# Block products summed in PSUM banks, and q's relu and weighting moved to GpSimd, in a fused attention and SwiGLU kernel

## The chip, the cores and the metric

The kernel runs on one core of one Trainium2 chip. The metric is the device time of one execution in microseconds. A core has TensorE (PE, matrix products), VectorE (DVE), ScalarE (ACT), GpSimd (POOL) and SyncE (SP, which here only issues transfers); each runs its own queue of instructions in order, and they wait for one another through semaphores. TensorE writes only into PSUM, eight banks of 128 partitions by 512 float32 values.

## The reference

Eight batches of eight heads, 576 positions, 64 features. A linear attention with cosine weights, whose result feeds a gated feed-forward network:

```python
theta = pi / 2 * arange(S) / S
phi(x) = concat([relu(x) * cos(theta), relu(x) * sin(theta)])   # 64 -> 128 features
q_p, k_p = phi(q), phi(k)
kv  = einsum('bhsf,bhsd->bhfd', k_p, v);   z = sum of k_p over s
x   = einsum('bhsf,bhfd->bhsd', q_p, kv) / (einsum('bhsf,bhf->bhs', q_p, z) + 1e-6)
g   = x @ w_gate                      # x as 4608 tokens of 512
out = (silu(g) * (x @ w_val)) @ w_out # 512 -> 1536 -> 512
```

## The kernel before

**Tokens and groups.** The 4608 tokens are taken in nine groups (`tg` = 0 to 8) of 512 tokens, four tiles `t` of 128 each. A batch has 576 tokens, four and a half tiles, so batches and groups drift apart. One group is twelve steps `ffn_fc(tg, fc)` and then the output product. A step multiplies the group's transposed tokens `xT[tg]` by 128 columns of the gate and of the value weights (L531: two PSUM banks, eight matmuls of 128x512), ACT takes silu of the one bank (L537), and DVE multiplies it by the other into `ht` (L542).

**The output by seven products.** For groups 2 to 8 `out_by_quarters` forms the output `ht @ w_out` as a two by two block product with seven block products in place of eight, in Winograd's form. Each `product` is 12 matmuls of 128x256 (L648) over six chunks. The sums of blocks of `ht` (S1 to S4) are formed by DVE in `token_sum` (L619), those of the weights (T1 to T4) once. In program order the products are: aq00·bq00 into bank `a`; S3·T3 into `e`; S2·T2 into `b`; aq10·bq10 on top of `a`; S1·T1 on top of `b`; aq11·T4 into `c`; S4·bq11 on top of `b`. The quarters of the output stand in SBUF tiles `ob` as C11, C12, C21 and C22. ACT copies `a` out twice, as C12 (L661, a part of the later sums) and as C11 (L672). `added` (L655) is DVE's scalar_tensor_tensor, PSUM times 2^-12 plus an SBUF block: five times in a group, C22 = e + C12, C21 = b + C22, C22 = b + C22, C21 = c + C21, C12 = b + C12. Each is a read of a bank that a later product may only write after it. In the last group `b` is two banks and its additions are halved.

**PSUM.** `take` hands out banks by least recent use; a bank with a `hold` stays taken until `give_back`.

**Attention work between the steps.** A plan written by hand (`at(slot, function)`) puts the attention's work for later batches into numbered slots, 16 for each group: twelve behind the `ffn_fc` steps, four inside the output product (`slot_of(0)` to `slot_of(3)`). For batches 4 to 7, in slots 12, 12, 13 and 14 of a group, `phi_q(b, g)` has ACT take relu of a quarter of q in place (L234) and DVE multiply it by the table of cosines and sines `tab` into `r_q` (L251; the tile pool `rel` has one buffer). In slots 15 and 16 SP issues `qturn_dma`: two transposing transfers of `r_q` into `phit` (L274). In slots 15 to 18 come relu of k (ACT, L234) and `vmul` (DVE, L255). The group 2 works for batch 4, group 3 for 5, group 4 for 6 and group 5 for 7. `a_tile2` (L415) multiplies `phit` by the state for the tiles of the next group, DVE normalises (`x_of`, L425 to L438), and SP transposes x into `xT` (L515).

**Loads.** POOL's queue issues the loads of q, k and v, 576 KB each. `load_behind(b)` first copies two values out of `phit` of batch b − 1 (L850), which makes POOL wait until those transposes have landed, and then issues q, k and v of batch b (L107). SP's queue holds the stores of `ob` (L570), the transposes L274 and the transposes L515, in that order from the end of one group to the next.

Of the kernel before, what the change touches and what calls it, by code (L numbers as in the profile page):

```python
# [11 lines left out]
BF16 = mybir.dt.bfloat16  # L12
FP16 = mybir.dt.float16
AF = mybir.ActivationFunctionType
ALU = mybir.AluOpType
# [3 lines left out]
def kernel(  # L19
# [10 lines left out]
    nc = tc.nc  # L30
    B, H, S, D = q.shape
    P = 128
    G = H // 2
    J = G // 2
    SH = 64
    NC = S // SH
# [9 lines left out]
    UP = float(2 ** 12)  # L46
    DOWN = 1.0 / UP
    HC = FC // 2
    HT = T // 2
    HD = d_model // 2  # L50
# [3 lines left out]
    rel = ctx.enter_context(tc.tile_pool(name="rel", bufs=1))  # L54
# [13 lines left out]
    now = [0]  # L68
    held = {}

    def take(n, hold=None):

        taken = {x for r in held.values() for x in r}
        free = [b for b in range(0, 8, n) if not any(b <= x < b + n for x in taken)]

        b0 = min(free, key=lambda b: (n == 1 and hold is not None and hold[0] == "o" and b ^ 1 not in taken,
                                      sorted(used[b:b + n], reverse=True)))
        if hold is not None:
            held[hold] = range(b0, b0 + n)
        touch(range(b0, b0 + n))  # L80
        return banks[:, b0] if n == 1 else banks[:, b0:b0 + n]

    def touch(r):
        now[0] += 1
        for x in r:
            used[x] = now[0]
# [5 lines left out]
    raws = {}  # L92
# [36 lines left out]
    first = {"q": lodge(G * QCUT * D, FP32).rearrange("p (g c d) -> p g c d", g=G, c=QCUT)}  # L129
# [25 lines left out]
    for j in range(2):  # L155
        t = consts.tile([P, 8 * J * D1], BF16, name=f"kvd_{j}")
# [8 lines left out]
    def idle_products(n, cols=P):  # L165
        ps = take(1)[:, 0:4 * cols]
        for _ in range(n):
# [22 lines left out]
                            op0=ALU.mult, op1=ALU.add)  # L190
# [4 lines left out]
    csk, cst = cs_all[:, 0], cs_all[:, 1]  # L195
# [7 lines left out]
        out=tab.rearrange("p c e d -> p (c e) d"),  # L203
        in_=csk.rearrange("p c e -> p (c e)").to_broadcast([P, NC * 2, D]),
    )
    v2s = []
    for j in range(2):
        t = consts.tile([P, G, NC, 2, W], BF16, name=f"v2_{j}")
# [21 lines left out]
    st = {}  # L230
# [14 lines left out]
    def phi_q(b, g):  # L245

        if g == 0:
            st[b, "q"] = rel.tile([P, G, NC, 2, D], BF16, name="r_q")
        o = raws[b, "q"][:, g]
        relu_op("act", o, o)  # L250
        nc.vector.tensor_tensor(out=st[b, "q"][:, g], in0=o.unsqueeze(2).to_broadcast([P, NC, 2, D]),  # L251
                                in1=tab, op=ALU.mult)

    def vmul(b, g):
        nc.vector.tensor_tensor(  # L255
# [262 lines left out]
    def ffn_mm(tg, fc, lo=0, hi=GH, which=(0, 1)):  # L518

        n = (hi - lo) * SH  # L520
        ts = slice(lo // 2, hi // 2)
        fs = slice(fc * P, (fc + 1) * P)
        if 0 in which:
            if 2 * n <= 512:
                both = take(1, ("f", tg, fc, lo))
                st["f", tg, fc, lo] = [both[:, 0:n], both[:, n:2 * n]]
            else:
                st["f", tg, fc, lo] = [take(1)[:, 0:n] for _ in range(2)]
        for i in which:
            for kc in range(KC):  # L530
                nc.tensor.matmul(out=st["f", tg, fc, lo][i], lhsT=(wg_sb, wv_sb)[i][:, kc, fs], rhs=xT[tg][:, ts, kc],  # L531
                                 start=(kc == 0), stop=(kc == KC - 1))
# [24 lines left out]
    o_ps = {}  # L557
# [23 lines left out]
    def ffn_out(t, f0=0, f1=None):  # L581

        f1 = FC if f1 is None else f1
        if f0 == 0:
            o_ps[t] = take(1, ("o", t))
        r = t % OUT * P
        for fc in range(f0, f1):
            nc.tensor.matmul(out=o_ps[t], lhsT=ht[:, fc, r:r + P], rhs=wo_sb[:, fc],  # L588
                             start=(fc == 0), stop=(fc == FC - 1))
        if f1 < FC:  # L590
            return
        ps = o_ps.pop(t)
        give_back(("o", t))
        if t % 2 == 0:
            nc.scalar.mul(out=ob_of(t), in_=ps, mul=DOWN)
        else:
            nc.vector.tensor_single_scalar(out=ob_of(t), in_=ps, scalar=DOWN, op=ALU.mult)
        store(t)


    aq = ht.rearrange("p (i w) (h t) -> p w h i t", w=2, h=2)
    bq = wo_sb.rearrange("p (i w) (h x) -> p w h i x", w=2, h=2)
    sums = consts.tile([P, 3, HC, HT], FP16, name="sums")
    S1, S2, S3, S4 = aq[:, 0, 1], sums[:, 0], sums[:, 1], sums[:, 2]
# [21 lines left out]
    def out_by_quarters(tg, slot_of):  # L626

        last = tg == NTG - 1
        t0 = tg * OUT
        for t in (t0, t0 + 2):  # L630
            ob_of(t)
        C11, C12 = (obs[t0 // 2][:, :, x * HD:(x + 1) * HD] for x in range(2))
        C21, C22 = (obs[t0 // 2 + 1][:, :, x * HD:(x + 1) * HD] for x in range(2))

        def home(nm, parts=1):
            return [take(1, ("o", tg, nm, i)).rearrange("p (t x) -> p t x", x=HD) for i in range(parts)]

        def free(nm, parts=1):
            for i in range(parts):
                give_back(("o", tg, nm, i))  # L640

        def at_of(x, i):
            return x[i][:, 0] if len(x) == 2 else x[0][:, i]

        def product(to, a, b, first):
            for i in range(2):
                for kc in range(HC):
                    nc.tensor.matmul(out=at_of(to, i), lhsT=a[:, kc, i * P:(i + 1) * P], rhs=b[:, kc],  # L648
                                     start=first and kc == 0 and (i == 0 or len(to) == 2),
                                     stop=kc == HC - 1, skip_group_check=True)  # L650

        def added(o, ps, x):
            for i in range(len(ps)):
                sl = slice(i, i + 1) if len(ps) == 2 else slice(0, 2)
                nc.vector.scalar_tensor_tensor(out=o[:, sl], in0=ps[i][:, 0:1] if len(ps) == 2 else ps[i],  # L655
                                               scalar=DOWN, in1=x[:, sl], op0=ALU.mult, op1=ALU.add)

        nb = 2 if last else 1
        a = home("a")
        product(a, aq[:, 0, 0], bq[:, 0, 0], True)  # L660
        nc.scalar.mul(out=C12, in_=a[0], mul=DOWN)  # L661
        e = home("e")
        product(e, S3, T3, True)
        added(C22, e, C12)
        b = home("b", nb)
        free("e")
        product(b, S2, T2, True)
        added(C21, b, C22)
        token_sum(4, 4, 6)
        slot_of(0)  # L670
        product(a, aq[:, 1, 0], bq[:, 1, 0], False)
        nc.scalar.mul(out=C11, in_=a[0], mul=DOWN)  # L672
        free("a")
        if last:
            store_two(t0, slice(0, HD))
        slot_of(1)
        product(b, S1, T1, False)
        added(C22, b, C22)
        if last:
            store_two(t0 + 2, slice(HD, d_model))  # L680
        c = home("c")
        product(c, aq[:, 1, 1], T4, True)
        added(C21, c, C21)
        free("c")
        if last:
            store_two(t0 + 2, slice(0, HD))
        else:
            for t in (t0 + 2, t0 + 3):
                store(t)
        slot_of(2)  # L690
        product(b, S4, bq[:, 1, 1], False)
        added(C12, b, C12)
        free("b", nb)
        for t in (t0, t0 + 1):
            store(t, *((slice(HD, d_model), (nc.sync, nc.scalar)) if last else ()))
        slot_of(3)
# [6 lines left out]
    hold = consts.tile([P, 1], FP32)  # L703
# [144 lines left out]
    def load_behind(b):  # L848

        nc.gpsimd.tensor_copy(out=hold2, in_=phit[b - 1][0:1, :, 0, 0, 0])  # L850
        load(b, "q")
        if b > 3:
            load_kv(b)

    def load_kv(b):
        for nm in ("k", "v"):
            load(b, nm)
# [7 lines left out]
    for b in range(2, B):  # L865
        s0 = SLOTS * (b - 1)
        keng = "dve" if b == 2 else "act"
        steps = [lambda b=b, g=g: phi_q(b, g) for g in range(G)]
        steps += [lambda b=b, g=g: (relu_k(b, g, g + 1, keng), vmul(b, g)) for g in range(G)]
        if b == 2:  # L870
            fs, tq = [s0 + i for i in (0, 0, 1, 1, 4, 5, 5, 6)], (s0 + 2, s0 + 2)
        else:
            p0 = s0 - SLOTS
            fs, tq = [p0 + 12, p0 + 12] + [p0 + 11 + i for i in range(2, 8)], (p0 + 15, p0 + 16)
            if b == 3:
                fs, tq = [p0 + 12 + i for i in range(4)] + [s0 + 4, s0 + 4, s0 + 5, s0 + 5], (s0 + 2, s0 + 2)
            at(p0 + 3 if b < 5 else p0 + 1, lambda b=b: load_behind(b))
        tk = (s0 + 4, s0 + {2: 8, 3: 7}.get(b, 5))
        for s, f in zip(fs, steps):
            at(s, f)  # L880
        for e in range(2):
            at(tq[e], lambda b=b, e=e: qturn_dma(b, e))
        at(tk[-1], lambda b=b: kv_mm(b), lambda b=b: kv_out2(b))
        at(tk[-1] + 1, lambda b=b: kv_free(b))
# [59 lines left out]
```

## Time and profile before

| | before |
|---|---|
| median of 3 runs | 318.63 us (318.44 to 318.73) |
| the profiled execution's own time | 318.28 us |
| its span from first to last instruction | 316.5 us |
| granted TensorE clock, mean | 0.999 |
| busy: PE, DVE, ACT, POOL | 308.6, 225.0, 130.1, 35.7 us |
| matmuls | 2624 |
| `added` on DVE (L655) | 38, 24.6 us |
| `phi_q` on DVE (L251), on ACT (L234, raw_q) | 24 each, 17.6 and 14.9 us |
| mean DMA | 130 GB/s |

All times in views of the trace count from the start of the span. A line of a busy group gives its source line, engine, operation, output and inputs with their shapes, how often it ran, total busy time and the mean of one in nanoseconds, and then the idle time of the engine before it with what ended it. A line of the chain or the timeline gives start, duration, engine and line. PE is the matmul, PEld the loading of weights ahead of it. Matmuls are pipelined: a product of 12 is issued in 1.31 us, and its result is there about 0.16 later than the last issue.

### The profile page before, as it was taken

How to read it: one execution, taken by the hardware profiler on the slowest of the kernel's cores; microseconds unless marked ns; L12 is line 12 of the kernel's file. 1: busy time of each engine (PE TensorE's matmuls, PEld its weight loads, DVE VectorE, ACT ScalarE, POOL GpSimd, SP SyncE). 2: the span in 40 equal slices, each digit the busy share in tenths (PEclk: the TensorE clock that was granted, in tenths of full speed). 3: DMA queues.
4: the chain of work that ended last, by engine and by line, in shares of the span. 5: the costliest groups of instructions: out<-in, count | busy, mean ns of one | idle time of the engine just before them, and what ended most of it. 6: DMA issues, size and time to landing. Idle time of an engine off the chain costs nothing.

```text
span 316.5 us, 6619 instructions
## 1 busy us (share of the span) xinstructions
PE 308.6 (98%) x2624; PEld 182.7 (58%) x2624; DVE 225.0 (71%) x448; ACT 130.1 (41%) x237; POOL 35.7 (11%) x60
## 2 busy tenths in 40 slices
PE   8899999999999999999999999999999999999994
PEld 4597455455445485548554855477456745774473
DVE  7873777797658898598858875888578437843662
ACT  7554545753435354334533343334432133213320
POOL 6754202000200200030003000300000000000000
PEclk9999999999999999999999999999999999999999
DMA  7999999998896985989497989598951241233004
GB/s 256 223 198 197 206 205 136 226 130 110 143 220 90 174 117 133 134 107 199 111 141 86 194 158 139 69 195 135 156 78 35 59 92 24 39 68 71 2 0 133
DMA packets 74766, 41.06 MB, mean 130 GB/s; under 512 B 49904, under 2 KB 69872, under 8 KB 74736
## 3 DMA queue, kind: packets, MB, share of 16 engines
q1 hardware_dynamic: 51952, 22.55, 40.1%
q0 software_dynamic: 22192, 17.57, 37.3%
q10 hardware_dynamic: 592, 0.52, 0.5%
q8 instruction: 20, 0.33, 0.4%
q14 instruction: 10, 0.08, 0.1%
HBM read 37.75 MB, written 9.44 MB: 149 GB/s over the span
## 4 chain that ended last, share of the span: by engine, by line
PE 92%; DMA 2%; DVE 2%; ACT 2%; issue 0%; ACTq 0%
PE banks L531 59%; PE banks L648 18%; PE banks L588 6%; PE banks L301 3%; PE banks L415 2%; DMA xT<-x 2%; PE banks L461 1%; PE banks L397 1%; DVE v L255 1%; PE banks L168 1%; PE banks L341 0%; PE banks L503 0%; ACT L200 0%; ACT phit L349 0%; ACT kvd L313 0%
## 5 line engine op out<-in xcount | busy, mean ns | idle before, releaser
L537 ACT ACTIVATE sg<-banks 128x512 bf16<-128x512 f32 (+2 forms) x116 | 65.8, 568 | 118.8 <-PE banks L531 111.3
L531 PE MATMUL banks<-xT,wg_sb 128*128 128x512 bf16 (+2 forms) x464 | 111.3, 364 | 0.6 <-DMA xT<-x 0.6
L542 DVE TENSOR_TENSOR ht<-sg,banks 128x512 f16<-128x512 bf16 (+2 forms) x116 | 74.5, 648 | 52.3 <-PE banks L531 45.3
L531 PE MATMUL banks<-xT,wv_sb 128*128 128x512 bf16 (+2 forms) x464 | 111.3, 364 | 0.0
L531 PEld LDWEIGHTS <-wv_sb 128*128 128x128 bf16 x464 | 44.9, 98 | 48.7
L531 PEld LDWEIGHTS <-wg_sb 128*128 128x128 bf16 x464 | 43.1, 98 | 42.3 <-issue 0.8
L655 DVE SCALAR_TENSOR_TENSOR ob<-banks,ob 128x512 f32<-128x512 f32 (+1 forms) x38 | 24.6, 648 | 14.4 <-PE banks L648 13.4
L648 PEld LDWEIGHTS <-ht 128*128 128x128 f16 x336 | 32.4, 98 | 3.9
L648 PEld LDWEIGHTS <-sums 128*128 128x128 f16 x252 | 24.6, 98 | 3.6 <-issue 0.8
L255 DVE TENSOR_TENSOR v<-raw_v,tab 128x1152 bf16<-128x1152 bf16 x31 | 22.7, 751 | 0.2 <-ACT raw_v L701 0.2
L588 PE MATMUL banks<-wo_sb,ht 128*128 128x512 f16 x96 | 22.7, 379 | 0.0
L438 DVE TENSOR_TENSOR x<-banks,rec 128x512 bf16<-128x512 f32 (+1 forms) x32 | 21.6, 674 | 1.3 <-PE banks L397 0.3
L648 PE MATMUL banks<-wo_sb,ht 128*128 128x256 f16 x168 | 20.6, 273 | 0.0
L648 PE MATMUL banks<-wt_sb,sums 128*128 128x256 f16 x168 | 19.5, 273 | 0.0
L648 PE MATMUL banks<-wt_sb,ht 128*128 128x256 f16 x168 | 19.5, 273 | 0.0
L251 DVE TENSOR_TENSOR r_q<-raw_q,tab 128x1152 bf16<-128x1152 bf16 x24 | 17.6, 752 | 2.7 <-ACT raw_q L234 2.4
L234 ACT ACTIVATE raw_k<-raw_k 128x576 bf16<-128x576 bf16 (+1 forms) x25 | 17.0, 694 | 0.0
L850 POOL COPY hold<-phit 1x2 bf16<-1x2 bf16 x5 | 1.2, 244 | 130.6 <-DMA phit<-r_q 130.6
L619 DVE TENSOR_TENSOR sums<-ht 128x1024 f16<-128x1024 f16 (+1 forms) x28 | 15.5, 552 | 0.2
L234 ACT ACTIVATE raw_q<-raw_q 128x576 bf16<-128x576 bf16 x24 | 14.9, 674 | 0.0
L588 PEld LDWEIGHTS <-ht 128*128 128x128 f16 x96 | 9.1, 98 | 8.9 <-issue 0.2
L415 PEld LDWEIGHTS <-phit 128*128 128x128 bf16 (+1 forms) x240 | 10.0, 100 | 6.5 <-issue 1.3
(95 smaller groups left out, 209.8 us busy)
## 6 DMA issues: line engine op xcount, KB each, us to landing
out_dram<-ob SPq DMA_DIRECT2D x67, 128.0 KB, 2.4
raw_k<-in_k_dram POOLq DMA_DIRECT2D x7, 576.0 KB, 9.3
raw_q<-in_q_dram POOLq DMA_DIRECT2D x6, 576.0 KB, 6.7
raw_v<-in_v_dram POOLq DMA_DIRECT2D x6, 576.0 KB, 11.7
wo_sb<-in_moe_w_out_dram POOLq DMA_DIRECT2D x3, 512.0 KB, 12.8
wg_sb<-in_moe_w_gate_dram POOLq DMA_DIRECT2D x5, 256.0 KB, 9.1
wv_sb<-in_moe_w_val_dram POOLq DMA_DIRECT2D x5, 256.0 KB, 9.4
wo_sb<-in_v_dram SPq DMA_DIRECT2D x2, 576.0 KB, 4.2
```

The costliest lines, as they stand in the source:

```text
L234: nc.scalar.activation(out=out, in_=in_, func=AF.Relu)
L251: nc.vector.tensor_tensor(out=st[b, "q"][:, g], in0=o.unsqueeze(2).to_broadcast([P, NC, 2, D]), in1=tab, op=ALU.mult)
L255: nc.vector.tensor_tensor(out=v2s[b % 2][:, g, :, :, 0:D], in0=(first if b == 0 and g == 0 else {"v": raw_of(b, "v")})["v"][:, g].unsqueez ...
L415: nc.tensor.matmul(out=ps[ms, e, g * D1:(g + 1) * D1], lhsT=phit[b][:, e, g, c:c + n].rearrange("p c s -> p (c s)"), rhs=kv2s[b % 2][:, e, ...
L438: nc.vector.tensor_tensor(out=st["x", t].rearrange("p (y e d) -> p e y d", e=2, d=D)[:, :, ys], in0=ps[:, :, 0:2 * J * D1].rearrange("p e ...
L531: nc.tensor.matmul(out=st["f", tg, fc, lo][i], lhsT=(wg_sb, wv_sb)[i][:, kc, fs], rhs=xT[tg][:, ts, kc], start=(kc == 0), stop=(kc == KC - 1))
L537: nc.scalar.activation(out=sg[:, 0:n], in_=st["f", tg, fc, lo][0], func=AF.Silu, scale=DOWN)
L542: nc.vector.tensor_tensor(out=ht[:, fc, r:r + n], in0=st.pop(("s", tg, fc, lo))[:, 0:n], in1=ps[1], op=ALU.mult)
L588: nc.tensor.matmul(out=o_ps[t], lhsT=ht[:, fc, r:r + P], rhs=wo_sb[:, fc], start=(fc == 0), stop=(fc == FC - 1))
L619: nc.vector.tensor_tensor(out=o[:, lo:hi], in0=x[:, lo:hi], in1=y[:, lo:hi], op=op)
L648: nc.tensor.matmul(out=at_of(to, i), lhsT=a[:, kc, i * P:(i + 1) * P], rhs=b[:, kc], start=first and kc == 0 and (i == 0 or len(to) == 2), ...
L655: nc.vector.scalar_tensor_tensor(out=o[:, sl], in0=ps[i][:, 0:1] if len(ps) == 2 else ps[i], scalar=DOWN, in1=x[:, sl], op0=ALU.mult, op1= ...
```

## The change

Two things are done together.

First, the sums of block products are formed in PSUM as far as they go. After product `a`, ACT copies bank `a` into bank `b`, and S2·T2 is then added on top of it by the matmuls themselves (no clearing flag). C22 is first e alone, scaled by ACT. DVE's scalar_tensor_tensor forms C22·2^12 + b and writes it into the PSUM bank `c`, on top of which aq11·T4 is added later. C21 is then a plain scaled copy of `c` by ACT, C12 a plain scaled copy of `b` by DVE, and C22 takes b once more as before. Banks that are to be added onto must have been written in full by a matmul (`seeded`, `fills` and the list `filled` in `take`). Four banks are held for a time where three were.

Second, for batches 4 to 7 `phi_q` goes. In its place `phi_q_whole(b)` is called at the end of `load_behind(b)`: 18 GpSimd instructions of 128 partitions by 4 x 64 values, one for each of the nine slots c and for cosine and sine, each max with 0 and product with a value per partition, from the raw q to `r_q`. They stand in POOL's queue behind the issues of that batch's loads.

```diff
+    filled = [False] * 8
-    def take(n, hold=None):
+    def take(n, hold=None, fills=False, seeded=False):
...
-        free = [b for b in range(0, 8, n) if not any(b <= x < b + n for x in taken)]
+        free = [b for b in range(0, 8, n) if not any(b <= x < b + n for x in taken)
+                and (filled[b] or not seeded)]
...
+        filled[b0:b0 + n] = [fills or seeded] * n
...
+    def phi_q_whole(b):
+        r_q = st[b, "q"] = rel.tile([P, G, NC, 2, D], BF16, name="r_q")
+        for c in range(NC):
+            for w in range(2):
+                nc.gpsimd.tensor_scalar(out=r_q[:, :, c, w], in0=raws[b, "q"][:, :, c], scalar1=0.0,
+                                        scalar2=csk[:, c, w:w + 1], op0=ALU.max, op1=ALU.mult)
...
         a = home("a", fills=True)
         product(a, aq[:, 0, 0], bq[:, 0, 0], True)
-        nc.scalar.mul(out=C12, in_=a[0], mul=DOWN)
-        e = home("e")
+        b = home("b", nb, seeded=True)
+        for p_, o_ in each(b, a[0]):
+            nc.scalar.copy(out=p_, in_=o_)
+        e = home("e", fills=True)
         product(e, S3, T3, True)
-        added(C22, e, C12)
-        b = home("b", nb)
+        nc.scalar.mul(out=C22, in_=e[0], mul=DOWN)
+        c = home("c", seeded=True)
         free("e")
-        product(b, S2, T2, True)
-        added(C21, b, C22)
+        product(b, S2, T2, False)
+        for p_, o_, x_ in each(b, c[0], C22):
+            nc.vector.scalar_tensor_tensor(out=o_, in0=x_, scalar=UP, in1=p_, op0=ALU.mult, op1=ALU.add)
         token_sum(4, 4, 6)
         slot_of(0)
         product(a, aq[:, 1, 0], bq[:, 1, 0], False)
-        nc.scalar.mul(out=C11, in_=a[0], mul=DOWN)
+        copied("act", C11, a)
...
         product(b, S1, T1, False)
-        added(C22, b, C22)
+        for p_, x_ in each(b, C22):
+            nc.vector.scalar_tensor_tensor(out=x_, in0=p_, scalar=DOWN, in1=x_, op0=ALU.mult, op1=ALU.add)
...
-        c = home("c")
-        product(c, aq[:, 1, 1], T4, True)
-        added(C21, c, C21)
+        product(c, aq[:, 1, 1], T4, False)
+        copied("act", C21, c)
...
         product(b, S4, bq[:, 1, 1], False)
-        added(C12, b, C12)
+        copied("dve", C12, b)
...
         load(b, "q")
         if b > 3:
             load_kv(b)
+            phi_q_whole(b)
...
-        steps = [lambda b=b, g=g: phi_q(b, g) for g in range(G)]
+        steps = [lambda b=b, g=g: phi_q(b, g) for g in range(G)] if b < 4 else [lambda: None] * G
```

`each` splits a pair of banks into its halves, and `copied` is a scaled copy of a bank by ACT (`mul`) or by DVE (`tensor_single_scalar`).

More of the change, by code (lines that the diff above doesn't have):

```diff
@@ L527, in ffn_mm @@
             else:
-                st["f", tg, fc, lo] = [take(1)[:, 0:n] for _ in range(2)]
+                st["f", tg, fc, lo] = [take(1, fills=n == 512)[:, 0:n] for _ in range(2)]
         for i in which:
@@ L584, in ffn_out @@
         if f0 == 0:
-            o_ps[t] = take(1, ("o", t))
+            o_ps[t] = take(1, ("o", t), fills=True)
         r = t % OUT * P
@@ L633, in out_by_quarters, with home @@
         C21, C22 = (obs[t0 // 2 + 1][:, :, x * HD:(x + 1) * HD] for x in range(2))
-        def home(nm, parts=1):
-            return [take(1, ("o", tg, nm, i)).rearrange("p (t x) -> p t x", x=HD) for i in range(parts)]
+        def home(nm, parts=1, **kw):
+            return [take(1, ("o", tg, nm, i), **kw).rearrange("p (t x) -> p t x", x=HD) for i in range(parts)]
         def free(nm, parts=1):
@@ L640, in free @@
                 give_back(("o", tg, nm, i))
-        def at_of(x, i):
-            return x[i][:, 0] if len(x) == 2 else x[0][:, i]
         def product(to, a, b, first):
@@ L647, in product, with each, copied @@
                 for kc in range(HC):
-                    nc.tensor.matmul(out=at_of(to, i), lhsT=a[:, kc, i * P:(i + 1) * P], rhs=b[:, kc],
-                                     start=first and kc == 0 and (i == 0 or len(to) == 2),
+                    nc.tensor.matmul(out=to[i][:, 0] if len(to) == 2 else to[0][:, i],
+                                     lhsT=a[:, kc, i * P:(i + 1) * P], rhs=b[:, kc],
+                                     start=first and kc == 0 and i == 0,
                                      stop=kc == HC - 1, skip_group_check=True)
[L652 to L656, printed above, removed]
+        def each(ps, *others):
+            if len(ps) == 1:
+                return [(ps[0], *others)]
+            return [(ps[i][:, 0:1], *(o[:, i:i + 1] for o in others)) for i in range(2)]
+        def copied(eng, o, ps, x=DOWN):
+            for p_, o_ in each(ps, o):
+                if eng == "act":
+                    nc.scalar.mul(out=o_, in_=p_, mul=x)
+                else:
+                    nc.vector.tensor_single_scalar(out=o_, in_=p_, scalar=x, op=ALU.mult)
         nb = 2 if last else 1
-        a = home("a")
+        a = home("a", fills=True)
         product(a, aq[:, 0, 0], bq[:, 0, 0], True)
-        nc.scalar.mul(out=C12, in_=a[0], mul=DOWN)
-        e = home("e")
+        b = home("b", nb, seeded=True)
+        for p_, o_ in each(b, a[0]):
+            nc.scalar.copy(out=p_, in_=o_)
+        e = home("e", fills=True)
         product(e, S3, T3, True)
-        added(C22, e, C12)
-        b = home("b", nb)
+        nc.scalar.mul(out=C22, in_=e[0], mul=DOWN)
+        c = home("c", seeded=True)
         free("e")
-        product(b, S2, T2, True)
-        added(C21, b, C22)
+        product(b, S2, T2, False)
+        for p_, o_, x_ in each(b, c[0], C22):
+            nc.vector.scalar_tensor_tensor(out=o_, in0=x_, scalar=UP, in1=p_, op0=ALU.mult, op1=ALU.add)
         token_sum(4, 4, 6)
```

## The prediction

> **What bounds the kernel now.** I read the page first: engine shares, then the chain that ended last.
>
> ```profile
> PE 308.6 (98%) x2624; PEld 182.7 (58%) x2624; DVE 225.0 (71%) x448; ACT 130.1 (41%) x237; POOL 35.7 (11%) x60
> PE 92%; DMA 2%; DVE 2%; ACT 2%; issue 0%; ACTq 0%
> ```
>
> TensorE is 98% busy at a granted clock of 0.999 and is 92% of the chain. The change leaves its matmuls alone (5,250 rows in the built programs of both). So work taken from DVE or ACT is worth nothing in itself: only the places where TensorE stands still can be won, and new ones are the danger. The chain in order of time has them:
>
> ```profile
> 143.47 7.86 PE banks L648 x72
> 151.36 1.47 PE banks L648 x12
> ...
> 178.61 7.27 DMA xT<-x
> 186.01 10.52 PE banks L531 x48
> ...
> 272.75 9.17 PE banks L648 x84
> ```
>
> Undisturbed, 84 quarter products take 9.17 us (0.109 each). The group ending at 152.83 has its last 12 set apart: there is a hole ahead of 151.36. The timeline there:
>
> ```profile
> 149.94 0.76 DVE L251 TENSOR_TENSOR r_q<-raw_q,tab 128x1152 bf16<-128x1152 bf16 x1 [0.15 <-ACT raw_q L234]
> 150.62 1.43 DVE L655 SCALAR_TENSOR_TENSOR ob<-banks,ob 128x512 f32<-128x512 f32 x2
> 151.36 1.47 PE L648 MATMUL banks<-wo_sb,sums 128*128 128x256 f16 x12
> 151.36 1.19 PEld L648 LDWEIGHTS <-sums 128*128 128x128 f16 x11 [0.21 <-issue]
> ```
>
> The last product (S4, bank b) may not write until DVE has read b into C22. That read could begin at 150.05 (S1's product issued by 149.85, plus 0.20, the distance everywhere here), but DVE is in `phi_q` until 150.62. TensorE loses 151.36 − 151.16 = 0.20. The same hole is at 118.97, 183.98 and 217.09, in the four groups that run `phi_q` for batches 4 to 7: **4 x 0.19 = 0.78 us**, all that `phi_q` costs TensorE. The three groups without it have none.
>
> A second hole: the group before 186.01 had issued its last product by 185.29 (183.98 + 12 x 0.109), so the next waited 0.72 us for its last xT transpose, issued at 178.61 and landing 7.3 later behind raw_v (issued 172.51, landing 13.0 later). raw_v's load waits on POOL (L850) for `phit` of batch 5, and that hangs on SP:
>
> ```profile
> 152.08 6.01 SPq L570 DMA_DIRECT2D out_dram<-ob  x8
> 158.20 8.12 SPq L274 DMA_TRANSPOSE phit<-r_q  x2
> ```
>
> The transposes stand behind eight stores, which start when C21 is done (152.05). So r_q may be late without harm until 158.2, and from there each microsecond is lost.
>
> **What the Trainium skill says.** PSUM — Partial Sum Buffer, "The four PSUM rules": ScalarE and VectorE writes leave the written bits alone, so a following matmul without the clearing flag adds onto what they put there. That is how the seeds work; no run so far shows it. SBUF — State Buffer, "Who interferes with whom": a DVE instruction with two SBUF inputs contends with a GpSimd instruction that reads SBUF, one blocking the other for its whole length; with at most one SBUF input it doesn't. Before, POOL has nothing but tiny copies there, so the trace can't tell. GPSIMD Engine Reference, "Elementwise — side-by-side cycle accounting": 1.03 cycles per element where reading and writing bound it, 2.6 for two inputs, at 1.2 GHz. POOL's rows:
>
> ```profile
> L158 POOL MEMSET kvd<- 128x520 f32 x1 | 0.5, 532 | 0.0
> masks.py:199 POOL TENSOR_SCALAR_AFFINE_SELECT ident<-ident 128x128 bf16<-128x128 bf16 x1 | 0.3, 294 | 0.1
> masks.py:197 POOL MEMSET ident<- 128x128 bf16 x1 | 0.2, 195 | 0.0
> L705 POOL COPY hold<-wo_sb 128x1 f32<-128x1 f32 x1 | 0.2, 185 | 1.9 <-DMA wo_sb<-in_v_dram 1.9
> ```
>
> The two memsets give (532 − 195)/(520 − 128) = 0.86 ns per element, 1.03 cycles: it agrees.
>
> **The change, part by part.**
>
> *q to POOL.* Gone: 16 ACT relus of 0.674 (10.8 us) and 16 DVE products of 0.752 (12.0 us). New: 4 x 18 POOL instructions of 128x256. No row shows one. Low: fixed 185 ns (the copy) + 256 x 0.86 = 0.40 us. High: the skill's two-input 2.6 cycles, 2.17 ns: 0.74 us. I take the select's slope, the nearest row that reads, computes and writes, (294 − 102)/127 = 1.5 ns (102 is POOL's 128x1 memset): **0.57 us, 10.2 us a batch**. They start when q has landed (issue plus 6.0 to 6.7: 109.0, 143.4, 177.8 and 209.0) and end at 119.2, 153.6, 188.0 and 219.2; SP reaches its transposes at 125.4, 158.2, 189.8 and 222.9. Hidden, with 1.8 us left in the tightest batch, 6; the low end only adds cover. What is late next if it isn't: `phit`, the next load, xT. On POOL the batch's k and v issues stand ahead of the 18, and the next L850 copy behind them waits for `phit` anyway. SP's order is untouched. The hole of 0.19 goes in all four groups, as C22 then finds DVE free: −0.78.
>
> *What of it arrives.* The start at 186.01 is set by the DMA chain, which begins with C21 of the group before. So only what is won ahead of C21 at 152.05 counts: 0.19 (at 118.97) plus C21 on ACT, 0.60 against 0.69: 0.09. What is won at 151.36 and 183.98 (0.39) is swallowed. After 186.01 the hole at 217.09 counts: 0.19. Sum **−0.47**; if that chain runs freer (SP's eight stores there took 6.01, 4.98 in the next group), up to 0.39 + 0.72 more.
>
> *The lock.* POOL's train overlaps token sums (L619, two SBUF inputs). In the group of 110.91, POOL begins at about 109.0 and four sums follow, at 109.57, 110.17, 112.25 and 112.71; each may wait for one POOL instruction, at most 0.57, and about 0.3 in the mean: 1.2 in all. S2's last part ends at 113.14 and is needed at 113.97, by the fifth matmul of the product begun at 113.53: 0.8 of slack, so about 0.4 lost, 1.5 if all wait fully, nothing if there is no such waiting. In the groups of 143.30 and 209.04 two sums follow, with 1.4 of slack (144.98 to 146.36): covered. I take **+0.3**. POOL, waiting for DVE in turn, ends perhaps 1 us later.
>
> *The sums in PSUM.* DVE has three instructions a group in place of five (last group six for eight), ACT four in place of two (five in the last): some 9 us off DVE and 9 onto ACT, both beside TensorE. The new waits, in the group of 143.30: TensorE's b product (145.92) waits for ACT's seed, 144.81 to 145.41 by the row L661 replaced: 0.5 of cover, ACT having idled 1.77 before. DVE's sum into c waits for C22 from ACT (146.12 to 146.72), which is there before b (147.43); it ends at 148.12, b's next product is at 148.54, token sum S4 behind it is needed at 151.6. C21 on ACT ends at 151.96; behind it the relu of k ends by 152.7, before the next silu at 153.79. The seeded banks are b = 4 and c = 5, as before, last read at 141.3 and 142.5. A write into PSUM in place of SBUF is the unseen cost: taken at the same 0.60 and 0.69, harmless up to 1.0 on ACT and 1.1 on DVE; quicker brings nothing. In the last group C12's copies take the scalar_tensor_tensor's place (0.69 by L597, 0.69 by L655) and the final stores hang on them: 0.
>
> Sum: −0.47 + 0.3 = about −0.2 on the profiled execution, whose own time is 318.28 (span 316.5 and 1.8 around it): 318.1. The median of the runs is 318.63, 0.35 above; so 318.4 there, and 318.2 with no lock, 317.1 with all swallowed gains freed.
>
> **The rivals.**
>
> *All holes close.* DVE's lighter queue and a freer DMA chain let 0.78 to 1.5 through: 317.1 to 317.9. For it: four identical holes of one cause. Against: the chain's piece of DMA at 178.61.
>
> *POOL is slow: the other side.* Place: batch 6, SP at 189.8. With 0.80 us an instruction its train takes 14.4 and, with 1 of lock waits, ends at 193.2, 3.4 late. `phit`, load and xT follow; xT landed 0.8 before it was needed (217.7 against 218.57), and the group now asks for it 0.19 sooner: 3.4 − 0.8 + 0.2 = 2.8 is lost. Batch 5 (143.4 + 15.4 = 158.8) loses 0.6 more. Net +2.9: **321.5**. It decides from (189.8 + 0.8 − 177.8 − 1)/18 = 0.66 us, and outweighs the gain from about 0.68, inside my bounds. Against it: the rows of POOL.
>
> *The lock starves DVE.* If the 18 pass as one block, the sums at 109.57, 144.10 and 209.8 wait some 9.5 us each, less 0.8 to 1.4 of slack: +25, about 344. Against it: the lock is held by the instruction.
>
> *Nothing moves:* the chain swallows all: 318.6.
>
> **How the numbers follow.** A measurement of this kernel can tell about 0.2%, 0.64 us, from no change. Near-zero case (my forecast, −0.47 with the lock's share): 0.32, of which little lies past a bound. Holes close: 0.26. POOL slow: 0.30. Starved: 0.05. Lock waits of more than 1 us, or a PSUM write that is too slow: 0.07. So faster 0.27, same 0.31, slower 0.42: the single likeliest mechanism is a small gain, but the price that decides the loss is the one that no row shows. The likeliest case's own range is 317.9 to 318.9. The whole range goes from 317.2 to 322.5: that leaves out the starved case, the worst of slow POOL and the last of the gains.
>
> **What would show it.** POOL's new row at 0.4 to 0.65 us; no hole before the seventh product at 119, 151, 184 and 217; SP's L274 still starting right behind its stores; the start near 186 still released by DMA xT. Wrong if POOL's row exceeds 0.7, if the L619 rows grow beyond 0.7 or their idle times name POOL, or if b's product waits for ACT.

## The result, and the profile after

| | before | after |
|---|---|---|
| median of the runs on one chip | 318.53 us (4; 318.00 to 318.73) | 340.27 us (4; 339.35 to 341.69) |
| ratio, 95% interval | | **1.0689 [1.0648, 1.073]** |
| profiled execution: time, span, granted clock | 318.28, 316.5, 0.999 | 339.35, 337.5, 0.974 |

The change makes the kernel 6.9% slower, 18 us past the upper end of the range. Ratios are of fast runs alone; one run of one experiment, the one that loads q early, was slow and is left out of that experiment's figures. From the page of the changed kernel: the engine shares, the granted clock in 40 slices, the chain by engine, and POOL's two rows (the number after the bar is total busy time, then the mean in ns, then POOL's idle time before such instructions).

```profile
PE 316.9 (94%) x2624; PEld 185.6 (55%) x2624; DVE 205.5 (61%) x418; ACT 129.1 (38%) x236; POOL 123.5 (37%) x132
...
PEclk9999999999999999989996999999899799999999
...
PE 47%; POOL 26%; DMA 16%; SPq 4%; DVE 3%; ACT 2%; issue 1%; POOLq 0%; ACTq 0%
...
L262 POOL TENSOR_SCALAR r_q<-raw_q,cs_all 128x256 bf16<-128x256 bf16 x72 | 87.7, 1231 | 17.1 <-DMA raw_q<-in_q_dram 17.1
...
L868 POOL COPY hold<-phit 1x2 bf16<-1x2 bf16 x5 | 1.1, 227 | 71.4 <-DMA phit<-r_q 71.4
```

TensorE was 92% of the chain and is now 47%; a quarter has become POOL's new instruction, which takes 1.23 us where the prediction had 0.57. The last line is the copy ahead of the loads: POOL's idle time before it was 130.6 us and is 71.4, so POOL now reaches it much later, after its train, and waits there only for the transposes of that train.

The chain in order of time (start, duration, piece):

```profile
102.38 6.21 DMA raw_q<-in_q_dram
108.80 22.47 POOL r_q L262 x18
131.29 3.61 SPq L285
134.94 6.93 DMA phit<-r_q
142.04 0.48 issue
142.53 6.41 DMA raw_q<-in_q_dram
149.11 22.05 POOL r_q L262 x18
171.18 3.45 SPq L285
174.67 7.18 DMA phit<-r_q
...
261.31 10.94 PE banks L656 x84
```

This is a **closed loop** through the attention work: q's load lands (6.4), POOL's train of 18 (22.3), SP's transposes (3.6) and their landing (7.1), and half a microsecond of copy and issue for the next batch's q: 40 us a turn. The copies ahead of the loads confirm it. Three before, and the last two of the same three after (the first, at 142.02, stands further down):

```profile
136.44 0.18 POOL L850 COPY hold<-phit 1x2 bf16<-1x2 bf16 x1 [31.93 <-DMA phit<-r_q]
...
170.53 0.18 POOL L850 COPY hold<-phit 1x2 bf16<-1x2 bf16 x1 [30.99 <-DMA phit<-r_q]
...
202.45 0.51 POOL L850 COPY hold<-phit 1x2 bf16<-1x2 bf16 x1 [29.18 <-DMA phit<-r_q]
```

```profile
182.00 0.17 POOL L868 COPY hold<-phit 1x2 bf16<-1x2 bf16 x1 [10.84 <-DMA phit<-r_q]
...
221.80 0.43 POOL L868 COPY hold<-phit 1x2 bf16<-1x2 bf16 x1 [10.91 <-DMA phit<-r_q]
```

Before, r_q was ready well ahead of SP, and SP's transposes came behind the stores of TensorE's own group, so TensorE set the pace, some 32.4 us for a group of 512 tokens. Now the loop does, for four batches running. The output product behind its last turn stood in the chain of before like this:

```profile
241.72 9.28 PE banks L648 x84
```

It starts at 261.31, **19.59 later**; its 84 matmuls take 10.94 instead of 9.28; what follows takes 0.25 less; that is the 21.0 by which the span grew.

TensorE itself loses the time in two ways. The timeline at the first wait:

```profile
141.92 0.30 PE L426 MATMUL banks<-kv,phit 128*128 128x65 bf16 x4 [2.48 <-DMA phit<-r_q]
...
142.02 0.18 POOL L868 COPY hold<-phit 1x2 bf16<-1x2 bf16 x1 [10.76 <-DMA phit<-r_q]
```

The brackets give the idle time before it and what ended it: TensorE and POOL wait for the same transpose. Such waits (2.67 at 141.92, 1.78 and 4.21 near 180, 1.34, 2.99 for xT, and 2.29 at 260.99) sum to 15.3 us; they are counted from where the issue of the matmul before ends, so they are about 0.2 longer than in the brackets. Then the clock falls. Two stretches right behind that wait (start and end, length, busy time and number on PE, PEld, DVE, ACT, POOL, granted clock, DMA share, GB/s):

```profile
142.10:146.30 4.20, 4.20 (x16) 1.53 (x13) 2.17 (x5) 0.60 (x1) 2.39 (x4) 0.59 0.77 111
146.30:150.00 3.70, 3.70 (x37) 2.92 (x36) 2.91 (x8) 1.17 (x2) 0.89 (x1) 1.00 1.18 190
```

Sixteen matmuls in 4.2 us at a clock of 0.59, where a 128x512 matmul is issued every 0.427 us instead of every 0.216: half pace. Then full pace again. Four such stretches, the dents in the PEclk line, add 7.4 us. 15.3 + 7.4, less the holes of before that closed (0.78 of `phi_q`, 0.72 at 186.01), is 21.2, against the 21.0 of the span.

What the prediction said of PSUM did happen. The timeline of the group that had its first hole at 118.97:

```profile
112.43 0.57 ACT L678 COPY banks<-banks 128x512 f32<-128x512 f32 x1 [1.83 <-PE banks L656]
112.72 0.65 DVE L630 TENSOR_TENSOR sums<-ht 128x512 f16<-128x512 f16 x1
...
115.13 0.69 DVE L686 SCALAR_TENSOR_TENSOR banks<-ob,banks 128x512 f32<-128x512 f32 x1 [0.72 <-PE banks L656]
...
117.67 0.69 DVE L697 SCALAR_TENSOR_TENSOR ob<-banks,ob 128x512 f32<-128x512 f32 x1 [1.52 <-PE banks L656]
...
118.78 1.47 PE L656 MATMUL banks<-wo_sb,sums 128*128 128x256 f16 x12
```

The last product (118.78) has no idle time before it: DVE waits for TensorE (1.52) and not the other way. The two writes into PSUM cost 0.57 and 0.69.

### The profile page after: what moved, and what is told of

It is laid out like the page before. It is cut to its first block, busy times and chain, and to the rows that moved or that the text cites. A ratio compares the mean times of both kernels' runs of the same rounds, so it can differ in the third digit from the quotient of the medians.

```text
span 337.5 us, 6645 instructions
## 1 busy us (share of the span) xinstructions
PE 316.9 (94%) x2624; PEld 185.6 (55%) x2624; DVE 205.5 (61%) x418; ACT 129.1 (38%) x236; POOL 123.5 (37%) x132
## 4 chain that ended last, share of the span: by engine, by line
PE 47%; POOL 26%; DMA 16%; SPq 4%; DVE 3%; ACT 2%; issue 1%; POOLq 0%; ACTq 0%
PE banks L542 28%; POOL r_q L262 26%; PE banks L656 9%; DMA phit<-r_q 8%; DMA raw_q<-in_q_dram 8%; PE banks L599 6%; SPq L285 4%; DVE v L266 1%; PE banks L426 1%; PE banks L312 1%; PE banks L472 1%; PE banks L408 1%; PE banks L172 1%; DVE ht L553 0%; PE banks L352 0%
## 5 line engine op out<-in xcount | busy, mean ns | idle before, releaser
L542 PE MATMUL banks<-xT,wg_sb 128*128 128x512 bf16 (+2 forms) x464 | 114.6, 373 | 2.8 <-DMA xT<-x 2.8
L542 PE MATMUL banks<-xT,wv_sb 128*128 128x512 bf16 (+2 forms) x464 | 113.9, 371 | 0.0
L262 POOL TENSOR_SCALAR r_q<-raw_q,cs_all 128x256 bf16<-128x256 bf16 x72 | 87.7, 1231 | 17.1 <-DMA raw_q<-in_q_dram 17.1
L542 PEld LDWEIGHTS <-wg_sb 128*128 128x128 bf16 x464 | 43.8, 99 | 46.8 <-issue 6.9
L656 PEld LDWEIGHTS <-sums 128*128 128x128 f16 x252 | 25.3, 101 | 3.6
L868 POOL COPY hold<-phit 1x2 bf16<-1x2 bf16 x5 | 1.1, 227 | 71.4 <-DMA phit<-r_q 71.4
L426 PE MATMUL banks<-kv,phit 128*128 128x65 bf16 (+1 forms) x240 | 12.7, 197 | 11.3 <-DMA phit<-r_q 11.3
L656 PE MATMUL banks<-wt_sb,sums 128*128 128x256 f16 x168 | 20.8, 283 | 0.0
L669 ACT ACTIVATE ob<-banks 128x512 f32<-128x512 f32 x14 | 8.4, 597 | 28.3 <-PE banks L656 28.3
## 6 DMA issues: line engine op xcount, KB each, us to landing
raw_v<-in_v_dram POOLq DMA_DIRECT2D x6, 576.0 KB, 11.4
```

Of the source, the lines that this page charges most:

```text
L262: nc.gpsimd.tensor_scalar(out=r_q[:, :, c, w], in0=raws[b, "q"][:, :, c], scalar1=0.0, scalar2=csk[:, c, w:w + 1], op0=ALU.max, op1=ALU.mult)
L426: nc.tensor.matmul(out=ps[ms, e, g * D1:(g + 1) * D1], lhsT=phit[b][:, e, g, c:c + n].rearrange("p c s -> p (c s)"), rhs=kv2s[b % 2][:, e, ...
L656: nc.tensor.matmul(out=to[i][:, 0] if len(to) == 2 else to[0][:, i], lhsT=a[:, kc, i * P:(i + 1) * P], rhs=b[:, kc], start=first and kc == ...
```

## The experiments

My theory: the train alone costs the time, by closing the loop; the PSUM sums are free. The rivals: the sums' waits cost it; POOL's lock slows DVE; the granted clock costs it.

**The two halves apart.** The first kernel is the changed one with `phi_q` back on ACT and DVE, the second the kernel before with the train alone.

```diff
-            phi_q_whole(b)
...
-        steps = [lambda b=b, g=g: phi_q(b, g) for g in range(G)] if b < 4 else [lambda: None] * G
+        steps = [lambda b=b, g=g: phi_q(b, g) for g in range(G)]
```

> The changed kernel with phi_q for batches 4 to 7 put back on ACT and DVE as in the kernel before; only the sums in PSUM stay. Theory (the POOL train alone costs the 21.7 us): 318.5 within 0.5, since DVE still has three phi_q products ahead of its second read of bank b and the holes of 0.19 us stay. Rival (the seeds and the write into bank c make TensorE wait): above 320, and b's product waits for ACT in the trace.

> The kernel before with only q's relu and weighting moved to POOL; the output sums as before. Theory (the train alone): 340 within 1.5, as the changed kernel. Rival (the two parts hurt each other, DVE and ACT being late for the seeds while POOL reads SBUF): clearly less than 340, by 3 us or more.

The sums alone: 318.28 us, 0.9991 [0.9982, 1.0]. The train alone: 340.12 us, 1.0668 [1.0646, 1.069]. So the train carries the whole loss, within the noise of these runs. With the sums alone the holes of 0.19 were still there (118.82, 151.21, 183.88 and 216.27). The chain by engine with the train alone, from its page, is that of the whole change:

```profile
PE 50%; POOL 25%; DMA 14%; SPq 4%; DVE 2%; ACT 2%; issue 1%; POOLq 0%; ACTq 0%
```

**What an instruction costs on POOL.** To the kernel before were added POOL instructions without use for the output, in several forms, behind the loads (L262 to L281 of that kernel):

```diff
+            for i in range(7):
+                nc.gpsimd.tensor_scalar(out=dum[:, :, i], in0=x[:, :, i], scalar1=0.0, scalar2=csk[:, i, 0:1], op0=ALU.max, op1=ALU.mult)
+            for i in range(7):
+                nc.gpsimd.tensor_scalar(out=dum[:, :, i], in0=x[:, :, i], scalar1=0.0, scalar2=0.5, op0=ALU.max, op1=ALU.mult)
...
+                nc.gpsimd.tensor_single_scalar(out=y[:, 256 * i:256 * i + 256], in_=z[:, 256 * i:256 * i + 256], scalar=0.0, op=ALU.max)
```

> The kernel before with extra POOL instructions behind the loads of batches 4 to 7, which read an old v and write a tile that nothing reads: the changed kernel's form, four runs of 64, with a value per partition; the same with two constants; 256 in one run with a value per partition; 256 with one operation and a constant; 64 and 512 elements in one run; a plain copy of 256; tensor_tensor of 256 and of 1152. The first should repeat 1.23 us. If the value per partition makes the price, the constant form falls to 0.6 or less; if the four short runs make it, one run of 256 does; if it is the instruction's arithmetic on bf16, all two-operation forms stay near 1.2, and 64 and 512 elements give a slope of some 4 ns per element. The skill's 2.6 cycles would give tensor_tensor of 1152 2.5 us.

The whole kernel took 325.43 us in one run. From the views of these lines in its trace: operation and number, shortest/median/longest in ns, first and last start, and shapes:

```profile
L262 POOL TENSOR_SCALAR dum<-raw_v,cs_all x7: 1128/1161/1448, 104.4 to 111.7; 128x256 bf16<-128x256 bf16 x7
...
L264 POOL TENSOR_SCALAR dum<-raw_v x7: 1054/1055/1561, 112.8 to 119.7; 128x256 bf16<-128x256 bf16 x7
...
L267 POOL TENSOR_SCALAR dum<-raw_v,cs_all x7: 1129/1148/1940, 141.8 to 149.3; 128x256 bf16<-128x256 bf16 x7
...
L269 POOL TENSOR_SCALAR dum<-raw_v x7: 834/841/1079, 150.6 to 155.8; 128x256 bf16<-128x256 bf16 x7
...
L272 POOL TENSOR_SCALAR dum<-raw_v,cs_all x6: 488/489/1066, 173.8 to 177.0; 128x64 bf16<-128x64 bf16 x6
...
L274 POOL TENSOR_SCALAR dum<-raw_v,cs_all x3: 1989/2237/2623, 177.6 to 181.8; 128x512 bf16<-128x512 bf16 x3
...
L276 POOL COPY dum<-raw_v x6: 394/399/935, 184.4 to 186.6; 128x256 bf16<-128x256 bf16 x6
...
L279 POOL TENSOR_TENSOR dum<-raw_v x7: 653/678/696, 205.9 to 209.6; 128x256 bf16<-128x256 bf16 x7
...
L281 POOL TENSOR_TENSOR dum<-raw_v,tab x2: 2344/2520/2697, 210.3 to 212.7; 128x1152 bf16<-128x1152 bf16 x2
```

L262 is the train's own form: max and product with a value per partition, on four runs of 64. One run of 256 (L267) costs the same, so the short runs are not it. Two constants in place of the value per partition (L264) save 0.1. One operation with a constant (L269) still costs 0.84, a copy (L276) 0.40. So it is **tensor_scalar itself**, and its second operation adds only some 0.2: from L272 to L267, (1148 − 489)/192 = 3.43 ns per element, and from L267 to L274, with 512 elements, more. A product of two tensors of the same size (L279) takes 0.68, less than tensor_scalar with one operation, though it reads twice as much. Why tensor_scalar costs this, no run shows. The Trainium skill's 2.6 cycles for two inputs (GPSIMD Engine Reference, "Elementwise — side-by-side cycle accounting") would be 2.5 us for 1152 elements, and L281 agrees; it just isn't the price of this instruction.

**A train short enough.** The changed kernel with only the nine cosine halves on POOL; the sine halves on DVE in `phi_q`'s slots, 9 instructions with a median of 0.30.

```diff
-            for w in range(2):
+            for w in range(1):
...
+    def phi_q_sin(b, g):
+        for c in range(2 * g, NC if g == G - 1 else 2 * g + 2):
+            nc.vector.tensor_scalar(out=st[b, "q"][:, :, c, 1], in0=raws[b, "q"][:, :, c], scalar1=0.0,
+                                    scalar2=csk[:, c, 1:2], op0=ALU.max, op1=ALU.mult)
...
```

> The changed kernel with half the train: POOL does the nine cosine instructions, DVE does the nine sine ones as tensor_scalar of 128x256 in the old slots of phi_q. Theory (the train is late at SP): 9 x 1.23 = 11.1 us from landing, so r_q is ready at 120, 154.5, 189 and 220, just ahead of SP's transposes: 318 to 319.5, about 21 us better than the changed kernel. If the cost were in proportion to POOL's work (lock, clock): about 329.

317.66 us, 0.9977 [0.9969, 0.9986]: the loss is gone, and a little is won, with half of the instructions still on POOL. So the cost isn't in proportion to POOL's work. Its timeline:

```profile
109.13 10.64 POOL L262 TENSOR_SCALAR r_q<-raw_q,cs_all 128x256 bf16<-128x256 bf16 x9 [4.47 <-PE banks L547]
...
126.03 3.61 SPq L290 DMA_TRANSPOSE phit<-r_q  x1
```

A train of 10.6 us, nearly the 10.2 of the prediction, ends at 119.8, 6 us before SP's transposes. This is the case that I had forecast, built with instructions half as many and twice as dear. None of the holes of 0.19 is left; TensorE waits for xT instead, 0.20 at 185.19 and 0.66 at 218.05.

**Where the threshold lies.** The same with 13 of the 18 on POOL.

```diff
-            for w in range(2):
+            for w in range(2 if c < 4 else 1):
...
```

> As the half train, but 13 of the 18 instructions on POOL and 5 on DVE: 13 x 1.23 = 16.0 us. Theory (deadline at SP): ready at 125, 159.4, 193.8 and 225 against 125.4, 158.2, 189.8 and 222.9, so batches 5 and 6 are late by 1.2 and 4.0: 321 to 324. Rival (loss in proportion to the instructions beyond nine): 13 of 18 give 22 x 4/9 = 9.8 more than the half train, 327.5.

321.32 us, 1.009 [1.0063, 1.0116]. Timeline:

```profile
144.70 16.41 POOL L262 TENSOR_SCALAR r_q<-raw_q,cs_all 128x256 bf16<-128x256 bf16 x13 [3.96 <-DVE sums L635]
...
161.13 8.58 SPq L290 DMA_TRANSPOSE phit<-r_q  x2
```

and chain:

```profile
178.32 8.26 DMA xT<-x
...
212.48 8.04 DMA xT<-x
```

SP now starts when POOL ends (161.11), not behind its stores, and the wait comes out where the rival of the prediction put it, at xT: 1.91 at 186.72 and 1.75 at 220.66. The copies stand at 137.93, 171.77 and 205.52, some 33.8 apart, so this loop too is longer than a group, by 1.4.

**Is it the loop or the clock?** In the changed kernel TensorE was given zero products ahead of the four tiles that wait, to keep it busy.

```diff
+        idle_products({18: 12, 22: 27, 27: 6, 31: 10}.get(t, 0)) if t in (18, 22, 27, 31) else None
```

> The changed kernel with products of zeros (128x512, 0.216 us each, written to a free bank and read by nobody) on TensorE ahead of the four tiles that wait for phit: 12, 27, 6 and 10 of them, filling most of each stall. In the changed kernel TensorE runs at half pace (0.427 us for a matmul of 512) for about 4 us behind each stall, 7.4 us in all. Theory (a loop through POOL, SP and DMA sets the time up to the last stall near 261, so only the slow stretch behind that one counts): about 1.7 us less than the changed kernel, 338.5. Rival (stalls and slow stretches add up on TensorE): about 7 less, 333.

339.05 us, 1.0649 [1.0609, 1.0689] to before. Half pace was gone except behind one wait that was not filled (5.19 at 235.16). Yet the last transpose of `phit` lands at 261.14, where it landed at 260.95 in the changed kernel: up to there the loop sets the time, and half pace lies inside its slack. Only the stretch behind the last wait lies outside, worth 1.66 us in the changed kernel. Here its 84 matmuls run at full pace:

```profile
262.50 9.28 PE banks L657 x84
```

But they start 1.19 later, as the zero products ran on past the landing, so little of the 1.66 shows: the intervals of the two kernels overlap.

And the loop shortened by one link: q is loaded right behind the train, ahead of the copy that waits for `phit`.

```diff
+        if b > 4:
+            load(b, "q")
...
-        load(b, "q")
+        if b < 5:
+            load(b, "q")
```

> The changed kernel with the load of q for batches 5 to 7 issued right behind the previous train on POOL, ahead of the copy that waits for phit; k and v stay behind it. The train is as long as before. Theory (the loop is train 22.3, SP's transposes 3.6, their landing 7.1, the copy and the issues, then q's landing 6.4: 40.2 us a batch against a group of 32.4): without q's landing the loop is about 34.8, and of the loss of 21.7 some 7 to 11 stay: 325 to 330. Rival (the loss comes from POOL's work itself, by the lock or the clock, not from the loop): 340.

328.16 us (325.75 to 330.35), 1.0299 [1.0251, 1.0348]: more than half of the loss is gone. Two of its trains in the timeline:

```profile
145.16 22.59 POOL L262 TENSOR_SCALAR r_q<-raw_q,cs_all 128x256 bf16<-128x256 bf16 x18
...
181.18 22.14 POOL L262 TENSOR_SCALAR r_q<-raw_q,cs_all 128x256 bf16<-128x256 bf16 x18
```

No idle time stands before them: q is there. These two are 36.0 us apart: the train, SP and the landing (11.4) and 2.1 from the copy to the next train (k's and v's issues). The turn before took 36.2 and the one behind 37.7, all still over 32.4.

**Another instruction on POOL.** The changed kernel, with ACT's relu in its old slots and POOL doing DVE's four long products with the table.

```diff
+    def phi_q_pool(b, g):
...
+        relu_op("act", o, o)
+        nc.gpsimd.tensor_tensor(out=st[b, "q"][:, g], in0=o.unsqueeze(2).to_broadcast([P, NC, 2, D]), in1=tab, op=ALU.mult)
...
-            phi_q_whole(b)
...
```

> The sums in PSUM, relu of q on ACT in its old slots, and the weighting on POOL as four tensor_tensor of 128x1152 a batch in place of 18 tensor_scalar. At the price measured beside the kernel before (2.34 to 2.70 us each) they take 10 us from about 113.6, 146.0, 178.5 and 210, ready at 123.6, 156, 188.5 and 220, ahead of SP's transposes: 317.5 to 318.5, some 22 us better than the changed kernel with the same work of weighting on POOL. Rival (any elementwise work on POOL of this volume is late or blocks DVE): above 325.

317.78 us, 0.9981 [0.9971, 0.9992]. Its POOL row:

```profile
L270 POOL TENSOR_TENSOR r_q<-raw_q,tab 128x1152 bf16<-128x1152 bf16 x16 | 40.2, 2540 | 32.0 <-ACT raw_q L238 32.0
```

10.2 us a batch for the same weighting (the relu is on ACT again), less than half of the train. Here the lock that the prediction speaks of does show. Token sums and `vmul` on DVE, shortest/median/longest in ns:

```profile
L637 DVE TENSOR_TENSOR sums<-ht,sums x14: 418/684/1964, 109.6 to 306.9; 128x1024 f16<-128x1024 f16 x7, 128x512 f16<-128x512 f16 x7
...
L273 DVE TENSOR_TENSOR v<-raw_v,tab x31: 745/753/2324, 6.1 to 225.0; 128x1152 bf16<-128x1152 bf16 x31
```

All twelve such instructions that began while POOL's product ran were longer: four sums with 1.91 to 1.96 in place of 0.42, eight `vmul` with 1.92 to 2.32 in place of 0.75. After 85 us the token sums take 37.1 us in all where they took 30.9 before, and `vmul` 26.0 where they took 15.0. The 17 us lie beside TensorE, DVE being at 70%.

**Where the gain of closed holes goes.** Without POOL, the holes of 0.19 close too if DVE's `phi_q` is moved to slots 12, 12, 14 and 14. Once in the kernel with the sums, once in the kernel before; and the half train without the sums.

```diff
-            fs, tq = [p0 + 12, p0 + 12] + [p0 + 11 + i for i in range(2, 8)], (p0 + 15, p0 + 16)
+            fs, tq = [p0 + 12, p0 + 12, p0 + 14, p0 + 14] + [p0 + 11 + i for i in range(4, 8)], (p0 + 15, p0 + 16)
```

> The sums in PSUM with q's work on ACT and DVE, but the last two quarters of phi_q moved from slots 13 and 14 to slot 14, behind DVE's second read of bank b. Theory (the hole of 0.19 us is DVE busy with the third phi_q product): the four holes close and the time falls by 0.5 to 0.8 against the sums alone: 317.6 to 318. Rival (something else holds bank b): the holes stay and the time is that of the sums alone, 318.3.

> The kernel before with nothing changed but the slots of phi_q's last two quarters for batches 4 to 7: 14 in place of 13 and 14. No sums in PSUM, nothing on POOL. Theory (the hole is DVE's order alone): the four holes of 0.19 us close as they did with the sums, 317.7 to 318.1. Rival (the sums in PSUM brought part of that gain): 318.3 or more.

> The kernel before with the half train alone: nine cosine instructions on POOL, nine sine ones as tensor_scalar on DVE, the output sums as before. If the gain of the half train over the kernel before comes from DVE being free at its second read of bank b: 317.6 to 318.0, as with the sums. If the sums carry it: 318.3 or more.

With the sums 317.73 us, 0.9973 [0.9958, 0.9989]. Without them 318.28, 0.9994 [0.9982, 1.0006], less than I expected. The half train without the sums: 318.05, 0.9991 [0.9981, 1.0001], between the cases. In all three the holes are gone; what differs is how much is given back. The chain of the kernel before with later slots:

```profile
146.37 7.09 DMA xT<-x
...
179.46 6.66 DMA xT<-x
...
212.02 7.10 DMA xT<-x
```

In each group TensorE now reaches the next group's first step sooner and waits there for xT (0.71, 0.31 and 0.81), which doesn't land sooner: the middle one at 186.12, and 185.88 before. With the sums the same waits are 0.98 and 0.23. Both pairs (0.9973 against 0.9994, 0.9977 against 0.9991) hint that the sums make xT a little sooner, and in the trace of the sums alone the wait of 0.72 is absent (one of 0.21 stands at 217.79). But the intervals overlap: that is not settled.

**Freeing that chain.** So the loads that xT stands behind were started sooner: in the kernel with the sums and the later slots, the copy ahead of the loads reads only the half of `phit` that the first of the two transposes writes.

```diff
-        nc.gpsimd.tensor_copy(out=hold2, in_=phit[b - 1][0:1, :, 0, 0, 0])
+        nc.gpsimd.tensor_copy(out=hold2[:, 0:1], in_=phit[b - 1][0:1, 0:1, 0, 0, 0])
...
```

> The sums in PSUM and phi_q in the later slots, and in load_behind the copy that holds POOL's loads back waits for the first half of phit alone, about 4 us sooner. Theory (what is left after the holes is the last xT transpose queued behind the load of v, 0.98 and 0.23 us at the starts near 186 and 218): the loads of batches 4 to 7 issue some 4 us sooner, v lands sooner, both waits go, and the time falls to about 316.8. Rival (the loads then slow the second half of phit's transposes, which tiles need 3 us after they land now): a wait at L426 ahead of those tiles, and 318 or more.

316.78 us, **0.9939 [0.992, 0.9958]**: the best of all, faster than both kernels. The copies stand at 132.18, 163.41 and 195.71 where they stood at 138.05, 169.65 and 201.87, and in the chain from 90 to 230 us there is nothing but TensorE:

```profile
175.51 9.17 PE banks L656 x84
184.68 10.36 PE banks L542 x48
...
207.71 9.17 PE banks L656 x84
```

The 84 products run unbroken, and the next group starts as they end (175.51 + 9.17 = 184.68). Before, that place was a hole of 0.19 and a wait of 0.72. Whether this step would do as much without the sums was not tested.

## Why the prediction was wrong, and what of it was right

**The step that failed is POOL's price.** "I take the select's slope … 0.57 us, 10.2 us a batch" measured a median of 1.135 and a mean of 1.23, some 22 us a batch. Worse, 0.74 was called the high end. It was the page's price for two inputs, put on an instruction with one input and two operations, as though reading set the cost; the price runs show that it doesn't, with 0.68 for two inputs (L279) against 0.84 for one input and one operation (L269) and 1.16 for the train's form (L262). With 1.23 the prediction's own sums point the right way: the first train ends at 109.0 + 22.2 = 131.2 (131.29 in the trace) against SP's 125.4. Its own sign of being wrong, a row of POOL above 0.7, came true.

**The rival's place was right, its way of adding up was not.** "POOL is slow" named the place (SP's transposes, then `phit`, the load and xT), and the train of 13 showed it there. But it took each train's start, and SP's arrival, as they stood before (and xT's landing as 217.7, where the trace has 217.86). With 1.23 its sum over the two batches that it counts is (166.6 − 158.2) + (201.0 − 189.8 − 0.8 + 0.2) = 8.4 + 10.6 = 19.0, close to what came, but by luck: at that price batches 4 and 7 are late too, by 6.8 and 9.3, and the same sum gives 35. In its place stands the period: each train starts from the transposes of the one before, so once a turn (40 us) is longer than the group (32.4), every turn adds to the last. The copies show it: 5.6, 11.5 and 19.4 us late. The last transposes land 25.7 late (260.95 against 235.23), of which 6.0 was slack, as TensorE came to them only at 241.27 before; that leaves the 19.6 of the result. The early load of q, which takes one link out of the loop and nothing else, won back 12 us.

**A near hit by chance.** The number nearest to 340 was the 344 of the starved rival. Its mechanism did not happen: DVE's token sums grew by 0.26 us in all.

**Right:** that TensorE is the bound and only its holes can be won; the four holes of 0.19 and their cause (they close in every kernel that takes DVE's `phi_q` out of C22's way, and stay where it is put back); that the xT chain swallows the gain (0.71, 0.31 and 0.81 given back); and that freeing it would let more through. I put all holes together at up to 1.5 us; the last kernel won 318.87 × 0.0061 = 1.9, interval 1.3 to 2.6.

**The lock:** +0.3 us of TensorE's time was forecast; from 100 us on every wait of TensorE in the changed kernel is for `phit` or xT, so none of that came directly. DVE's token sums grew by 0.26 in all (30.91 to 31.17), nearly all of it in the one at 112.72, from 0.42 to 0.65. Yet 25 token sums and `vmul` began while an instruction of the train ran, and the other 24 took their usual time. As the prediction describes the lock, each would have been blocked. For POOL's product of two tensors that is what came, twelve times of twelve; for the train's instruction the measurement says otherwise. That DVE makes some of POOL's instructions longer (shortest 1.128, longest 1.744) is likely, but was not tested: all 16 above 1.2 overlap such a DVE instruction, but so do 17 shorter ones.

**The sums in PSUM** were forecast free, with 0.60 and 0.69 for the writes: 0.57 and 0.69, and 0.9991 alone. That they work at all bears out what the Trainium skill says of seeds (PSUM — Partial Sum Buffer, "The four PSUM rules"), for banks that a matmul had written in full.

**The chances** leaned the right way (slower, 0.42), but the range ended where the wrong upper price ended.

## What to carry to other kernels

Where work is moved to an engine whose instruction no row shows, bound its price by measuring that very form, operations and operand kinds included; a price for another form is no upper bound. Then ask whether the moved work lies on a loop from one batch to the next: if a turn becomes longer than the stage that it feeds, every turn adds the difference, and the loss is more than one lateness. And a hole that closes on the bound engine may be worth little (0.9994 here) until the transfer that ends next (xT behind the loads) is made sooner too.

## What was not expected of the hardware

- On POOL a tensor_scalar of 128x256 bf16, with two operations (1.15 us) or with one (0.84), costs more than a product of two tensors of that size (0.68); with two it costs almost three times a copy (0.40).
- Each wait of 2.3 to 4.2 us on TensorE in the changed kernel was followed by some 3 to 5 us at half pace (0.427 for a 128x512 matmul in place of 0.216); those of 1.34 and 1.78 were not. But in the kernel with q loaded early two close together (1.71 and 1.84) were, and in the kernel with the train alone one of 2.83 (at 142.10) was not, so the length of a wait doesn't decide alone. The Trainium skill (TensorE: Matmul & The Clock Gate, "What's actually happening") gives an idle window of about 3.4 us as the condition: the half pace agrees, but here waits of less than that were enough.
- POOL's products of two tensors slowed DVE's instructions with two SBUF inputs by 17 us in all; its tensor_scalar train, busy twice as long, lengthened DVE's token sums by 0.3.
